# A decode kernel's first load, split between two issuing engines

## The chip, the cores and the metric

The kernel runs on one core of one Trainium2 chip, in float32. The metric is the device time of the program in microseconds (us). Engines are called by their names and by the profile's short ones: TensorE (PE), VectorE (DVE), ScalarE (ACT), GpSimd (POOL), SyncE (SP). Loads are issued by SyncE or ScalarE and are carried out by sixteen DMA engines that both share; in the profile SyncE's loads are on queue q1, ScalarE's on q10.

## The reference, cut to what matters

One token for each of two sequences goes through attention over a cache of 4096 positions (32 heads of 128) and, beside it, through an MLP; a gate mixes the two.

```python
# x (2,1,576), k_cache and v_cache (2,32,4096,128), wq (576,4096), wo (4096,576),
# w1 (576,4608), b1 (4608), w2 (4608,576), b2 (576), gate_w (576)
g = sigmoid((x * gate_w).sum(-1, keepdims=True))
q = (x @ wq).reshape(B, 1, 32, 128).transpose(0, 2, 1, 3)
p = softmax(einsum("bhqd,bhkd->bhqk", q, k_cache) * 128 ** -0.5)
a = einsum("bhqk,bhkd->bhqd", p, v_cache).transpose(0, 2, 1, 3).reshape(B, 1, 4096) @ wo
b = gelu(x @ w1 + b1) @ w2 + b2          # tanh form of gelu
return g * a + (1 - g) * b
```

Each of the caches is 134 MB and each of its bytes is used once.

## The kernel before, in words

Three buffers of on-chip memory, `slots[0]`, `slots[1]` and `slots[2]`, hold 128 partitions of 64 KB each, 8 MB a buffer. All large loads go through them, and all of them are issued by SyncE in one hand-written order. A small class, `Order`, writes the waits: `op` and `dma` take the keys that an instruction reads (`r`) and writes (`w`), and wait for the last semaphore value of each key; `o.wrote` remembers it. A load raises its semaphore by 16 when all of it has landed.

At the start, ScalarE issues four small loads: x (two rows, key `xg`), gate_w (one row beside x, `gt_in`), b1 (`b1T`, 144 B in each of 128 partitions) and b2 (`b2r`, one row). SyncE meanwhile issues five large ones: the first 512 rows of wq into slot 0 (key `s0`; partition p takes rows 4p to 4p+3, which is one contiguous run of 64 KB), the last 64 rows of wq into the end of slot 1 (`s1q`), and w1 in three parts into slots 1 and 2 (`s1a`, `s2a`, `s2h`).

GpSimd makes an identity matrix. VectorE, when x and gate_w are there, copies a part of them (L176); TensorE transposes x and gate_w (`turn`, L183); VectorE writes `xq`, `xT` and `gT` from the result (L190 to L193). TensorE then runs, in this order: the gate's products (`gate`, L198), q from slot 0 (`q_whole`, L241, reads `xq` and `s0`), q from the last rows (`q_half`), b2's part of the output (`bias2`, L267), and the MLP's first layer (L282, L291). VectorE and ScalarE finish the MLP's activation (L300 to L314).

SyncE's next load, the first K tile in two halves (`k_load(0)`), goes into slot 0 and so waits until TensorE is through with `q_whole`; the second K tile, into slot 1, waits for the MLP's products, the first V tile, into slot 2, for the rest of the MLP.

The main loop has sixteen steps (2 sequences x 8 groups of 4 heads). In each, VectorE multiplies the K tile by q (L353) and sums (L355), takes the maximum (L356 to L358), ScalarE takes the exponentials (L365), TensorE multiplies by the V tile (L384). K tiles alternate between slots 0 and 1, V tiles use slot 2; each load is issued as soon as its slot is free. After the loop w2 and wo come through the same slots, in seven loads; the semaphores of the early loads, listed in `early`, are used a second time there (value 32). TensorE adds their products (L473), VectorE copies (L492), TensorE adds the last rows of wo (L506), VectorE copies once more (L510) and the output is stored.

Of the kernel before, what the change touches and what calls it, by code (L numbers as in the profile page):

```python
# [8 lines left out]
PE = mybir.EngineType.PE  # L9
# [3 lines left out]
class Order:  # L13
# [50 lines left out]
    def op(self, e, f, r=(), w=(), extra=(), sig=None):  # L64

        self.wait(e, self.deps(r, w) + list(extra))
        ins = f(self.eng[e])
        if sig is not None:
            ins.then_inc(sig, 1)
            return None  # L70
        self.count[e] += 1
        ins.then_inc(self.sem[e], 1)
        t = self.token(e, self.sem[e], self.count[e])
        self.note(t, r, w)
        return t

    def dma(self, e, out, in_, r=(), w=(), extra=(), sem=None, val=16):
        self.wait(e, self.deps(r, w) + list(extra))
        if sem is None and self.spare:
            sem, val = self.spare.pop(0)  # L80
        elif sem is None:
            sem = self.tc.alloc_semaphore(f"d{self.nd}")
            self.nd += 1
        self.eng[e].dma_start(out, in_).then_inc(sem, 16)  # L84
        t = (None, sem, val, dict(self.seen[e]))
        self.note(t, r, w)
        return t


def kernel(tc, *args):  # L90
    with tc.tile_critical():
        stored = body(tc, *args)

    with tc.tile_critical():
        for own, sem, val, had in stored:
            tc.nc.sync.wait_ge(sem, val)


def body(tc, x, k_cache, v_cache, wq, wo, w1, b1, w2, b2, gate_w, out):
# [3 lines left out]
    F = w1.shape[1]  # L103
# [5 lines left out]
    NX = D // P  # L109
    XR = NX * P  # L110
    WQ = H * DH
# [6 lines left out]
    DW = D // 2  # L118
    SCALE = float(DH) ** -0.5
    SLOT = R * DH  # L120
    N1 = NQ - 1

    def sb(name, *shape):
        return nc.alloc_sbuf_tensor(name, list(shape), F32).ap()

    slots = [sb(f"slot{i}", P, SLOT) for i in range(3)]
    bank = [nc.alloc_psum_tensor(f"bank{i}", [P, 512], F32).ap() for i in range(8)]
# [3 lines left out]
    o = Order(tc)  # L131
    op, dma = o.op, o.dma
    S2 = ["s2a", "s2h", "s2r", "s2t", "xg", "b2r", "xe", "g1z"]


    b1T = sb("b1T", P, FR)
    spare = slots[2][:, 2 * F + 2 * FJ:]
    xg, spare = spare[:B + 1, :D], spare[:, D:]
    b2r, spare = spare[:1, :D], spare[:, D:]
# [1 line left out]
    dma("ACT", xg[B:B + 1], gate_w[None, :], w=["gt_in"])  # L141
    dma("ACT", b1T, b1.rearrange("(p r) -> p r", r=FR), w=["b1T"])
    dma("ACT", b2r, b2[None, :], w=["b2r"])


    hrow1 = w1[:XR].rearrange("(p r) n -> p (r n)", r=NX)
    wqh = slots[1][:, SLOT - WQ // 2:]
    FA = 3
    dma("SP", slots[0], wq[:XR].rearrange("(p r) n -> p (r n)", r=NX), w=["s0"])
    dma("SP", wqh, wq[XR:].rearrange("q (e n) -> (q e) n", e=2), w=["s1q"])  # L150
    dma("SP", slots[1][:, :FA * F], hrow1[:, :FA * F], w=["s1a"])
    dma("SP", slots[2][:, :F], hrow1[:, FA * F:], w=["s2a"])
    w1h = slots[2][:, F:F + F // 2]
    dma("SP", w1h, w1[XR:].rearrange("q (e n) -> (q e) n", e=2), w=["s2h"])
    early = [o.wrote[k][0][1] for k in ("xg", "gt_in", "b1T", "b2r", "s0", "s1q", "s1a", "s2a", "s2h")]
    hr = slots[2][:, 2 * F:2 * F + FJ]
    ht = slots[2][:, 2 * F + FJ:2 * F + 2 * FJ]

    def quad(src, i):
        g, b = divmod(i, B)  # L160
        return src[b, g * HQ:(g + 1) * HQ].rearrange("h (p r) d -> (h p) (r d)", p=HP)
# [26 lines left out]
    xq = sb("xq", P, NC6, B)  # L188
# [67 lines left out]
            ins = q_mm(e, NX + s, wqh, s, True)  # L256
        return ins

    op("PE", q_whole, r=["xq", "s0"], w=["q"])
    op("PE", q_half, r=["xq", "s1q"], w=["q"])  # L260


# [12 lines left out]
    def mlp_whole(lo, hi):  # L275
        def f(e):
            for c in range(lo, hi):
                t = slots[1][:, c * F:(c + 1) * F] if c < FA else slots[2][:, :F]
                for m in range(3):
                    for j in range(4):  # L280
                        at = j * FJ + m * FC
                        ins = e.matmul(hps[m][32 * j:32 * j + 32, :FC], xT[:, c], t[:, at:at + FC],  # L282
                                       start=(c == 0), stop=False, skip_group_check=True)
            return ins
        return f
# [8 lines left out]

    op("PE", mlp_whole(0, FA), r=["xT", "s1a"], w=["avp", "cps", "fin"])
    op("PE", mlp_whole(FA, NX), r=["xT", "s2a"], w=["avp", "cps", "fin"])
    op("PE", mlp_half, r=["xT", "s2h"], w=["avp", "cps", "fin"])

    for m, k in enumerate(("avp", "cps", "fin")):
# [5 lines left out]
       r=["s2r0", "s2r1", "s2r2"], w=["s2t"])  # L305
# [29 lines left out]
    def k_load(i):  # L335
        s = i % 2
        if i == 0:
            free = o.deps([], ["s0"])
            for a, sem in ((0, ksem[0]), (1, k0b)):
                c = slice(a * RH * DH, (a + 1) * RH * DH)  # L340
                dma("SP", slots[0][:, c], quad(k_cache, 0)[:, c], w=[f"s0{a}"], extra=free, sem=sem)
            return
        w = ["s0"] if s == 0 else ["s1a", "s1q", "s1"]
        dma("SP", slots[s], quad(k_cache, i), w=w, sem=ksem[s], val=16 * (i // 2 + 1))
# [15 lines left out]
    def soft(i):  # L360
        j = i % 2
        o.wait("ACT", o.deps([f"nm{j}", f"st{j}"], ["pt", "rs"]))
        for h in range(HQ):
            a = slice(HP * h, HP * (h + 1))
            ins = nc.scalar.activation(pt[a, h:R * HQ:HQ], stt[j][a], AF.Exp, bias=nmt[j][a], accum_out=rs[a])  # L365
        ins.then_inc(exps, 1)

    def gather(i):

        g, b = divmod(i, B)  # L370
        j = i % 2
        nc.scalar.wait_ge(avd, i + 1)
        nc.scalar.copy(avs, avp).then_inc(avc, 1)  # L373
        a = slice(32 * (g // 2), 32 * (g // 2) + 32)
        nc.scalar.wait_ge(cmb, i + 1)

        op("ACT", lambda e: e.copy(oS[a, b, g % 2], cps[a, :DH + 1]), r=[f"st{j}", f"nm{j}"], w=[f"oS{i}"])  # L377

    def quad_products(e, v, vin):
        e.wait_ge(exps, 1).then_inc(exps, -1)  # L380
        e.wait_ge(vin, 16).then_inc(vin, -16)  # L381
        for t in range(NT):
            j = t % 4
            ins = e.matmul(avp[32 * j:32 * j + 32], pt[:, 16 * t:16 * t + 32], v[:, 512 * t:512 * (t + 1)],  # L384
                           start=(t < 4), stop=(t >= NT - 4))
        ins.then_inc(avd, 1)
        e.wait_ge(avc, 1).then_inc(avc, -1)  # L387
        for rr in range(4):
            e.matmul(cps[:, :DH], sel[:, rr], avs[:, rr * DH:(rr + 1) * DH],  # L389
                     start=(rr == 0), stop=(rr == 3), skip_group_check=True)  # L390
        e.matmul(cps[:, DH:DH + 1], hsel, rs, start=False, stop=True, skip_group_check=True).then_inc(cmb, 1)  # L391


    WA = SLOT // D
    views = {"w2": w2.rearrange("(p r) n -> p (r n)", r=FR), "wo": wo.rearrange("(p r) n -> p (r n)", r=OR)}
# [7 lines left out]


    k_load(0)
    k_load(1)
    o.wait("SP", o.deps([], S2 + ["gt_in", "s2r0", "s2r1", "s2r2"]))
    nc.sync.dma_start(slots[2], quad(v_cache, 0)).then_inc(vin, 16)
    for i in range(NQ):
        qk(i)  # L410
        if i < NQ - 2:
            k_load(i + 2)
        elif i < N1:

            o.wait("SP", o.deps([], ["s0"]))
            nc.sync.dma_start(slots[0], quad(v_cache, N1)).then_inc(vlast, 16)
        soft(i)
        if i < N1:
            gather(i)
            nc.sync.wait_ge(avd, i + 1)  # L420
            if i < NQ - 2:
                nc.sync.dma_start(slots[2], quad(v_cache, i + 1)).then_inc(vin, 16)
    o.wait("PE", o.deps(["sel0", "sel1", "sel2", "sel3", "hsel", "pt"], ["avp", "cps"]))
    with nc.Fori(0, N1, engines=[PE], head_slot={PE: 0}):
        quad_products(nc.tensor, slots[2], vin)
    quad_products(nc.tensor, slots[0], vlast)
    gather(N1)

# [19 lines left out]
    for gp in range(2):  # L448
# [11 lines left out]
       r=["orr", "rg"], w=["oT"])  # L460
# [82 lines left out]
```

## Time and profile before

| | us |
|---|---|
| median of 3 runs (723.55 to 723.66) | 723.56 |
| the profiled execution | 723.58 |
| its span in the profile | 721.7 |
| VectorE busy | 573.1 |
| TensorE busy | 223.1 |
| ScalarE busy | 49.5 |

The span runs from the first to the last thing that the profile shows; the rest of the execution's time lies around it. The profile's DMA row gives, in 40 equal slices of the span or of a window, the mean busy share of the sixteen DMA engines in tenths; the GB/s row counts a packet's bytes in the slice in which it starts. A packet is one contiguous piece that one DMA engine moves; a 64 KB run is one packet. In section 3 the last figure of a queue is the time of its packets as a share of sixteen engines over the stretch. A row of the timeline gives start, duration, engine, line and operation, and in brackets how long the engine had been idle and what released it. Nearly all loads are issued from one line of the helper `Order.dma` (L84), so they are told apart by their tensors.

### The profile page before, as it was taken

Reading aid. Unit: us, or ns where it says so; the run is one execution under the profiler, and the core shown is the slowest. Engines: PE = TensorE matmul, PEld = TensorE weight load, DVE = VectorE, ACT = ScalarE, POOL = GpSimd, SP = SyncE. Lnnn points to the kernel's source line nnn. Section 1 sums busy time; section 2 is a strip of 40 time slices with the busy share of each in tenths; the row PEclk is TensorE's granted clock in tenths of the full one; section 3 lists DMA queues with packets and bytes.
Section 4 is the critical chain, followed back from the end, with each engine's and each line's share of the span. In section 5 each row is a group of like instructions: output and inputs, shape, how many; then the busy total and the mean of one; then the engine's idle time right before and its main releaser. Section 6 shows DMA issues by size and latency. Waiting matters only on the chain. (4 is left out here: it accounts for less than half of the span.)

```text
span 721.7 us, 4080 instructions
## 1 busy us (share of the span) xinstructions
PE 223.1 (31%) x1784; PEld 80.2 (11%) x1784; DVE 573.1 (79%) x124; ACT 49.5 (7%) x166; POOL 0.7 (0%) x6
## 2 busy tenths in 40 slices
PE   1790005050504032140505060504032130506556
PEld 1130002010101010010101020201001010102112
DVE  2007999999989898989899898989898989899100
ACT  0000010101010101010100001010101010100100
POOL 0000000000000000000000000000000000000000
PEclk9996557575666657575757575656657575757759
DMA  9999999999999999999999999999999999999996
GB/s 408 412 411 455 418 454 418 454 418 454 414 444 429 432 432 421 447 421 450 421 447 425 443 425 443 421 432 436 421 450 421 447 425 447 421 443 429 434 407 278
DMA packets 6656, 308.69 MB, mean 428 GB/s; under 512 B 876, under 2 KB 884, under 8 KB 1016
## 3 DMA queue, kind: packets, MB, share of 16 engines
q1 hardware_dynamic: 6488, 308.55, 99.0%
q8 instruction: 6, 0.10, 0.1%
q10 hardware_dynamic: 160, 0.03, 0.0%
q14 instruction: 2, 0.02, 0.0%
HBM read 308.57 MB, written 0.00 MB: 428 GB/s over the span
## 5 line engine op out<-in xcount | busy, mean ns | idle before, releaser
L353 DVE TENSOR_TENSOR slot<-slot,bank 128x16384 f32<-128x16384 f32 (+1 forms) x17 | 275.7, 16215 | 43.4 <-DMA slot<-in_A_k_cache_dram 43.4
L384 PE MATMUL bank<-slot,pt 128*32 128x512 f32 x1024 | 146.1, 735 | 448.4 <-PEq L381 448.4
L355 DVE TENSOR_REDUCE st<-slot 128x128 f32<-128x16384 f32 x16 | 275.5, 17220 | 0.6
L384 PEld LDWEIGHTS bank<-slot,pt 128*32 128x32 f32 x1024 | 40.2, 132 | 541.8 <-issue 541.8
L365 ACT ACTIVATE pt<-st,nm 32x128 f32<-32x128 f32 x64 | 33.0, 515 | 115.5 <-DVE nm L358 114.7
L373 ACT COPY avs<-bank 128x512 f32<-128x512 f32 x16 | 9.4, 585 | 437.7 <-PE bank L384 437.7
L304 DVE STREAM_TRANSPOSE slot<-slot 128x1152 f32<-128x1152 f32 x1 | 2.2, 2205 | 37.5 <-ACT slot L300 37.5
L492 DVE COPY pt<-bank 128x288 f32<-128x288 f32 x1 | 0.5, 458 | 31.3 <-PE bank L473 31.3
L241 PE MATMUL bank<-slot,xq 128*32 128x512 f32 x160 | 20.2, 669 | 7.9 <-DMA slot<-in_A_wq_dram 7.9
L389 PE MATMUL bank<-avs,sel 128*128 128x128 f32 x128 | 18.1, 284 | 12.7 <-PEq L387 12.7
L389 PEld LDWEIGHTS bank<-avs,sel 128*128 128x128 f32 x128 | 15.5, 191 | 26.8 <-issue 26.8
L473 PE MATMUL bank<-slot,hg 128*2 128x288 f32 x144 | 12.0, 478 | 8.4 <-DMA slot<-in_B_w_dram 8.4
L365 ACT ACTIVATION_READ_ACCUMULATOR pt<-st,nm 32x1 f32 x64 | 12.5, 195 | 0.0
L449 DVE TENSOR_TENSOR avs<-oS,dm 128x256 f32<-128x256 f32 x2 | 0.8, 422 | 14.5 <-ACT oS L377 14.5
L473 PE MATMUL bank<-slot,oT 128*2 128x288 f32 x108 | 9.9, 516 | 4.8 <-DMA slot<-in_A_wo_dram 4.8
L282 PE MATMUL bank<-slot,xT 128*32 128x384 f32 x96 | 7.9, 487 | 0.0
L241 PEld LDWEIGHTS bank<-slot,xq 128*32 128x32 f32 x160 | 5.2, 121 | 22.1 <-issue 14.1
L176 DVE COPY slot<-slot 3x64 f32<-3x64 f32 x2 | 0.4, 184 | 8.9 <-DMA slot<-in_gate_w_dram 8.9
L473 PEld LDWEIGHTS bank<-slot,hg 128*2 128x2 f32 x144 | 4.0, 95 | 15.5 <-DMA slot<-in_B_w_dram 8.4
L377 ACT COPY oS<-bank 32x129 f32<-32x129 f32 x16 | 4.1, 258 | 22.9 <-PE bank L391 22.9
L356 DVE TENSOR_REDUCE mx<-st 128x1 f32<-128x128 f32 x16 | 4.6, 286 | 0.5
L391 PEld LDWEIGHTS bank<-rs,hsel 128*128 128x128 f32 x32 | 4.9, 192 | 0.0
(59 smaller groups left out, 43.0 us busy)
## 6 DMA issues: line engine op xcount, KB each, us to landing
slot<-in_A_k_cache_dram SPq DMA_DIRECT2D x2, 4096.0 KB, 25.8
slot<-in_B_w_dram SPq DMA_DIRECT2D x1, 8064.0 KB
slot<-in_B_w_dram SPq DMA_DIRECT2D x1, 6912.0 KB, 41.0
slot<-in_B_w_dram SPq DMA_DIRECT2D x2, 2304.0 KB, 25.4
slot<-in_A_wo_dram SPq DMA_DIRECT2D x1, 4032.0 KB
slot<-in_A_wo_dram SPq DMA_DIRECT2D x1, 2304.0 KB
slot<-in_A_wo_dram SPq DMA_DIRECT2D x1, 1440.0 KB, 33.5
slot<-in_B_w_dram SPq DMA_DIRECT2D x1, 1152.0 KB
```

The lines of the kernel that those rows point to most:

```text
L241: ins = e.matmul(qps[b][m][HP * h:HP * (h + 1)], xq[:, c, b:b + 1].to_broadcast([P, HP]), v[:, :, h], start=(c == 0), stop=last, skip_grou ...
L282: ins = e.matmul(hps[m][32 * j:32 * j + 32, :FC], xT[:, c], t[:, at:at + FC], start=(c == 0), stop=False, skip_group_check=True)
L353: op(V, lambda e, lo=lo, hi=hi: e.tensor_mul(k[:, lo:hi], k[:, lo:hi], q.unsqueeze(1).to_broadcast([P, hi - lo, DH])), r=["q", key], w=[key])
L355: op(V, lambda e: e.tensor_reduce(stt[j], k, AX.X, ALU.add), r=[s] + [p[2] for p in parts], w=[f"st{j}"])
L356: op(V, lambda e: e.tensor_reduce(mxt, stt[j], AX.X, ALU.max), r=[f"st{j}"], w=["mx"])
L365: ins = nc.scalar.activation(pt[a, h:R * HQ:HQ], stt[j][a], AF.Exp, bias=nmt[j][a], accum_out=rs[a])
L373: nc.scalar.copy(avs, avp).then_inc(avc, 1)
L377: op("ACT", lambda e: e.copy(oS[a, b, g % 2], cps[a, :DH + 1]), r=[f"st{j}", f"nm{j}"], w=[f"oS{i}"])
L384: ins = e.matmul(avp[32 * j:32 * j + 32], pt[:, 16 * t:16 * t + 32], v[:, 512 * t:512 * (t + 1)], start=(t < 4), stop=(t >= NT - 4))
L389: e.matmul(cps[:, :DH], sel[:, rr], avs[:, rr * DH:(rr + 1) * DH], start=(rr == 0), stop=(rr == 3), skip_group_check=True)
L391: e.matmul(cps[:, DH:DH + 1], hsel, rs, start=False, stop=True, skip_group_check=True).then_inc(cmb, 1)
L473: ins = e.matmul(acc[64 * s + 32 * u:64 * s + 32 * u + B], lhs[:, r], wrow[name, r][0][:, u * DW:(u + 1) * DW], start=False, stop=r >= hi ...
```

## The change

ScalarE's first instruction is now a load of wq: partitions 0 to 15 of slot 0, sixteen runs of 64 KB (key `s0f`). SyncE loads the other 112 runs (key `s0`). x, gate_w, b1 and b2 follow on ScalarE behind the wq runs, in the same order as before. The large loads are written ahead of the small ones in the program; SyncE's order of its own is the same. `q_whole` and the first K load wait on both keys, and the semaphore of `s0f` comes first in the list of those used again at the end.

```diff
+    NE = 16
...
+    hrow1 = w1[:XR].rearrange("(p r) n -> p (r n)", r=NX)
+    wqh = slots[1][:, SLOT - WQ // 2:]
+    FA = 3
+
+    hrowq = wq[:XR].rearrange("(p r) n -> p (r n)", r=NX)
+    dma("ACT", slots[0][:NE], hrowq[:NE], w=["s0f"])
+    dma("SP", slots[0][NE:], hrowq[NE:], w=["s0"])
+    dma("SP", wqh, wq[XR:].rearrange("q (e n) -> (q e) n", e=2), w=["s1q"])
...
     dma("ACT", xg[:B], x.rearrange("b s d -> (b s) d"), w=["xg"])
     dma("ACT", xg[B:B + 1], gate_w[None, :], w=["gt_in"])
     dma("ACT", b1T, b1.rearrange("(p r) -> p r", r=FR), w=["b1T"])
     dma("ACT", b2r, b2[None, :], w=["b2r"])
-    hrow1 = w1[:XR].rearrange("(p r) n -> p (r n)", r=NX)
-    wqh = slots[1][:, SLOT - WQ // 2:]
-    FA = 3
-    dma("SP", slots[0], wq[:XR].rearrange("(p r) n -> p (r n)", r=NX), w=["s0"])
-    dma("SP", wqh, wq[XR:].rearrange("q (e n) -> (q e) n", e=2), w=["s1q"])
...
-    early = [o.wrote[k][0][1] for k in ("xg", "gt_in", "b1T", "b2r", "s0", "s1q", "s1a", "s2a", "s2h")]
+    early = [o.wrote[k][0][1] for k in ("s0f", "xg", "gt_in", "b1T", "b2r", "s0", "s1q", "s1a", "s2a", "s2h")]
...
-    op("PE", q_whole, r=["xq", "s0"], w=["q"])
+    op("PE", q_whole, r=["xq", "s0f", "s0"], w=["q"])
...
     def k_load(i):
         s = i % 2
         if i == 0:
-            free = o.deps([], ["s0"])
+            free = o.deps([], ["s0f", "s0"])
```

More of the change, by code (lines that the diff above doesn't have):

```diff
@@ L133, in body @@
     S2 = ["s2a", "s2h", "s2r", "s2t", "xg", "b2r", "xe", "g1z"]
+    hrow1 = w1[:XR].rearrange("(p r) n -> p (r n)", r=NX)
[5 more added lines that the diff above has]
+    dma("SP", wqh, wq[XR:].rearrange("q (e n) -> (q e) n", e=2), w=["s1q"])
+    dma("SP", slots[1][:, :FA * F], hrow1[:, :FA * F], w=["s1a"])
+    dma("SP", slots[2][:, :F], hrow1[:, FA * F:], w=["s2a"])
+    w1h = slots[2][:, F:F + F // 2]
+    dma("SP", w1h, w1[XR:].rearrange("q (e n) -> (q e) n", e=2), w=["s2h"])
     b1T = sb("b1T", P, FR)
@@ L143, in body @@
     dma("ACT", b2r, b2[None, :], w=["b2r"])
-    hrow1 = w1[:XR].rearrange("(p r) n -> p (r n)", r=NX)
-    wqh = slots[1][:, SLOT - WQ // 2:]
-    FA = 3
-    dma("SP", slots[0], wq[:XR].rearrange("(p r) n -> p (r n)", r=NX), w=["s0"])
-    dma("SP", wqh, wq[XR:].rearrange("q (e n) -> (q e) n", e=2), w=["s1q"])
[L151 to L154, printed above, removed]
-    early = [o.wrote[k][0][1] for k in ("xg", "gt_in", "b1T", "b2r", "s0", "s1q", "s1a", "s2a", "s2h")]
+    early = [o.wrote[k][0][1] for k in ("s0f", "xg", "gt_in", "b1T", "b2r", "s0", "s1q", "s1a", "s2a", "s2h")]
     hr = slots[2][:, 2 * F:2 * F + FJ]
```

## The prediction

> **What bounds the kernel now.** The page comes first: the profiled execution took 723.58 us, 0.02 above the median of the runs (723.56), 1.88 of it outside the span. The sum below is made against 723.58.
>
> ```profile
> span 721.7 us, 4080 instructions
> ...
> DMA  9999999999999999999999999999999999999996
> ...
> q1 hardware_dynamic: 6488, 308.55, 99.0%
> ...
> HBM read 308.57 MB, written 0.00 MB: 428 GB/s over the span
> ```
>
> The sixteen DMA engines are full from the first slice to the last but one, and q1, SyncE's queue, carries nearly every byte. VectorE, busiest of the compute engines, waits for K inside its main loop (view of waits), and the chain that ends last is a load, three short steps ahead of the output:
>
> ```profile
> DVE slot L353 <- DMA slot<-in_A_k_cache_dram: 43.4, 14, 3.4
> ```
> ```profile
> 680.76 35.82 DMA slot<-in_A_wo_dram
> ...
> 716.62 1.45 PE bank L506 x40
> ...
> 718.10 0.31 DVE pt L510
> ```
>
> So the kernel is a stream of bytes: it ends when the slowest DMA engine has moved its share. One engine moves 428/16 = 26.75 GB/s, and a 64 KB run takes it 65,536 B / 26.75 GB/s = 2.45 us. Since the queue never empties, an engine that starts earlier ends earlier, and an engine held up in the first load is late to the end. The start, in 20 ns slices (window 1.80 to 2.60), and what was issued:
>
> ```profile
> GB/s 0 0 230 0 0 0 0 0 0 13107 3277 0 0 0 3277 0 6554 6554 0 3277 0 3277 0 0 0 0 3277 0 3277 0 0 0 3277 0 0 0 0 0 3277 0
> ...
> q1 hardware_dynamic: 16, 1.05, 390.7%
> ```
> ```profile
> 0.91 0.55 ACTq L84 DMA_DIRECT2D slot<-in_A_x_dram  x1
> ...
> 0.95 0.86 SPq L84 DMA_DIRECT2D slot<-in_A_wq_dram  x2
> ...
> 2.61 1.28 ACT L204 ACT_TABLE_LOAD   x1 [2.61 <-issue]
> ```
>
> A packet counts in the slice where it starts: 3277 GB/s is one 64 KB run, 13107 four, 230 the two packets of x. ScalarE's x is issued at 0.91 and starts at 1.85, 0.94 later; SyncE's wq is issued at 0.95 and its first runs start at 1.98, the sixteenth engine's at 2.55. Those first runs take 3.907 x 0.80 x 16 / 16 = 3.13 us each, 0.68 over the steady 2.45.
>
> **The change, part by part.** (1) The start. If ScalarE's sixteen runs come 0.94 us after 0.91, they start at 1.85: 0.13 us sooner for the first engine, 0.70 for the last. If its issue is the slower one (x's took 0.55, the two on SyncE 0.86/2 = 0.43 each), SyncE's runs simply go first, as now. Bounds 0 and -0.70; I take **-0.30**, nearer to the mean than to the last engine.
>
> (2) The shape of the loads, which is the part that decides. Before, every large load covers 128 partitions, eight runs for each engine. After, sixteen engines write at one time into sixteen neighbouring partitions, and SyncE's 112 runs are seven for each engine. No row of before shows a large load narrower than 128. If 26.75 GB/s belongs to the engine, the sixteen runs cost 2.45 us whatever their address: 0. If it belongs to the memory side in proportion to partitions, sixteen of them get 428 x 16/128 = 53.5 GB/s, and 1.05 MB takes 19.6 us: +17.2. Between the ends lie two engines to one entrance (+2.45) and four (+7.35). The nearest rows are small ones, x (two engines, partitions 0 and 1, at once) and gate_w (one engine alone, with one packet of b1 in its window):
>
> ```profile
> q10 hardware_dynamic: 3, 0.00, 23.4%
> ```
> ```profile
> q10 hardware_dynamic: 2, 0.00, 4.2%
> ```
>
> The first window is 0.15 us long (from 1.80), the second 0.16 (from 7.80). x's packets took 0.234 x 16 x 0.15 = 0.56 us, gate's 0.042 x 16 x 0.16 = 0.11: five times as much for the pair, 2.6 times for each packet. It could be the cold start alone, since the first wq runs, on 128 partitions, are 0.68 over their steady time too; that is why the free end keeps a chance. I take a factor of 4, between 2.6 and 5: **+7.35 us**, both ends kept. [...]
>
> (3) SyncE's 112 runs. [...] One shared run costs 2.45, all seven 17.2. I take one: **+2.45**.
>
> Nothing behind makes these up: the bytes are the same, and the stretch from 60 to 400 us already runs full.
>
> ```profile
> 40.00:50.00 10.00, 10.00 (x108) 3.75 (x104) 0.00 (x0) 0.00 (x0) 0.00 (x0) 1.00 0.96 405
> ...
> 60.00:400.00 340.00, 83.02 (x592) 29.63 (x592) 316.17 (x47) 25.36 (x88) 0.00 (x0) 0.62 1.00 434
> ```
>
> (The last two columns are the DMA share and GB/s.)
>
> (4) x, gate_w, b1 and b2 behind the run on ScalarE's queue. Who waits:
>
> ```profile
> 10.79 0.40 DVE L176 COPY slot<-slot 3x64 f32<-3x64 f32 x2 [8.88 <-DMA slot<-in_gate_w_dram]
> ...
> 12.84 2.29 PE L198 MATMUL bank<-xT,gT 128*128 128x2 f32 x10 [0.74 <-DVE gT L193]
> 15.17 0.17 ACT L204 ACTIVATE gb<-bank 128x2 f32<-128x2 f32 x1 [11.27 <-PE bank L198]
> ...
> 17.85 0.21 DVE L233 TENSOR_TENSOR fsel<-ident 128x2 f32<-128x2 f32 x2
> 23.04 20.18 PE L241 MATMUL bank<-slot,xq 128*32 128x512 f32 x160 [7.91 <-DMA slot<-in_A_wq_dram]
> ...
> 39.86 10.86 SPq L84 DMA_DIRECT2D slot<-in_A_k_cache_dram  x3
> ...
> 55.54 2.21 DVE L304 STREAM_TRANSPOSE slot<-slot 128x1152 f32<-128x1152 f32 x1 [37.47 <-ACT slot L300]
> ...
> 59.61 0.23 DVE L314 TENSOR_TENSOR hg<-gt,g 128x72 f32<-128x72 f32 x1
> 60.84 8.69 DVE L353 TENSOR_TENSOR slot<-slot,bank 128x8192 f32<-128x8192 f32 x1 [1.00 <-DMA slot<-in_A_k_cache_dram]
> 70.86 8.69 DVE L353 TENSOR_TENSOR slot<-slot,bank 128x8192 f32<-128x8192 f32 x1 [1.33 <-DMA slot<-in_A_k_cache_dram]
> ```
>
> Small packets alternate with SyncE's runs on an engine. gate_w gets four entries ahead of it: the run, its semaphore, x and x's semaphore, 4 x 2.45 = 9.8 us at full rate. L176 moves from 10.79 to 20.6, and TensorE, which does the gate's products before q and is through with them 12.84 + 2.29 - 10.79 = 4.34 us after L176 starts, is ready for q at 24.9 instead of waiting from 15.13 for wq at 23.04: 1.9 late. With the runs shared, the run ahead costs 9.8 alone and one shared round 2.45: L176 at 10.79 + 9.8 + 7.35 + 2.45 = 30.4, TensorE ready at 34.7, wq there at 23.04 + 9.5 = 32.5, 2.2 late. The cover: K is issued at 39.86, when q's matmuls have freed slot 0, while wq and w1, all issued by 3.5 us, are 9.44 + 10.62 = 20.06 MB and keep the engines busy to 2.0 + 46.9 = 48.9. K may come 9 us later before a DMA engine idles. On VectorE the MLP ends 1.00 us ahead of the first half of K, and the second half is waited for by another 1.33, so 2.3 us late is absorbed there. I cost it at 0; without the cover, 1.9 to 2.2 us. VectorE's other work of the start (10.79 to 18.06) moves along and has until 55 us. b1 and b2 go later by the same entries; b2 is read after q, past 43 us, b1 after the MLP.
>
> (5) Instructions. One DMA issue more on ScalarE (0.24 to 0.55 us): the table load moves from 2.61 to 3.2 at most, its use is at 15.17 and moves later. One wait more ahead of q on TensorE, hidden as above. K's wait is on the same token of TensorE. The semaphores reused at the end shift by one place in the list: 0. The load of w2 and wo keeps its shape.
>
> **Sum:** 723.58 - 0.30 + 7.35 + 2.45 + 0 = 733.08, **733.1 us**, 1.3% slower.
>
> **The rivals.** (a) Not slower: addresses cost nothing, the engines are the limit. For it: the steady rate is one figure per engine in every stage of the stream, and x's slow pair has a second explanation. Against it: nothing wide could show the difference. Time: 723.58 - 0.30 = 723.3, within 722.9 and 723.6. The point that decides is whether the first sixteen runs take 3.1 us or near 10. [...]
>
> (b) The runs are shared, but less: SyncE's first runs get between ScalarE's on half the engines, so that two, not four, meet at a time over two rounds, and the 112 do not collide. 2 x 2.45 = 4.9: 723.58 - 0.30 + 4.9 = 728.2. For it: 0.91 and 0.95 are only 0.04 apart, so the order on each engine is open. Against it: x did come 0.13 sooner than wq.
>
> (c) The gate's chain runs past its cover: more than 9 us beyond the load's own delay, as when each small entry waits for two runs instead of one (7.35 more, still under 9). Each us above counts in full; 736 at 3 us more. Against it: gate_w and its semaphore came through by 10.79 with three runs ahead of them.
>
> (d) Faster by over 0.2%: 1.45 us is twice all that the start has to give (0.70).
>
> **How the numbers follow.** 0.2% of 723.56 is 1.45 us, about what a measurement of this kernel can tell from no change. The forecast, shared runs with some collisions among the 112 (729 to 737), has 0.53; (b), 725 to 729, 0.17; (a) 0.25; (c) 0.03; (d) 0.02. Slower: 0.53 + 0.17 + 0.03 = 0.73; same 0.25; faster 0.02. The range reaches from (a), 723.0, to the forecast's upper part, 737.0 (ScalarE's runs +7.35 and about two and a half shared runs, 6.1, each engine); the forecast's own range is 729 to 737.
>
> **What would show it.** In the profile of after: step 1, the slice in which the first 64 KB runs start (1.85 right, 1.98 wrong); step 2, the share of q10's sixteen runs (65,536 B at 3.1 us each would refute the sharing, near 10 confirm it) and GB/s over 2 to 20 us (near 410 or under 300); step 3, wq's landing, 23.04 before at the first L241, near 32.5 forecast, near 30 if the 112 do not collide; step 4, L176's start at 20 to 31 and a DMA share near 1 from 40 to 60 us in spite of it. The prediction is wrong if the first L241 starts near 23 us, or if the delay at L241 does not reappear at the end.

## The result, and the profile after

The changed kernel took 744.50 us (median of 4 runs, 743.98 to 744.95) against 723.61 for the kernel before (four runs beside it): ratio 1.0288, 95% interval 1.0275 to 1.0301. The forecast, 733.1, had the sign and the place of the loss, wq's arrival, but less than half of its size: 9.5 us were summed and 20.9 measured.

The page of the changed kernel, its span, DMA, GB/s and HBM rows:

```profile
span 742.9 us, 4082 instructions
...
DMA  9989999999999999999999999999999999999996
GB/s 169 265 347 418 445 434 434 430 438 438 427 434 431 434 434 434 430 434 434 430 441 427 430 445 427 427 445 427 427 448 427 434 438 430 434 434 434 428 413 262
...
HBM read 308.57 MB, written 0.00 MB: 415 GB/s over the span
```

The same bytes, and DMA engines that look as busy as before; only the GB/s row tells that in the first two slices (37 us) they move 169 and 265 where the later ones move some 430. A busy share counts a packet that is held up as busy. The timeline of the first 62 us has the delay where TensorE starts on q, and the chain that ends last has it again, unchanged, at the end:

```profile
37.84 0.40 DVE L180 COPY slot<-slot 3x64 f32<-3x64 f32 x2 [35.93 <-DMA slot<-in_gate_w_dram]
...
44.32 17.88 PE L245 MATMUL bank<-slot,xq 128*32 128x512 f32 x152 [2.14 <-DMA slot<-in_A_wq_dram]
...
59.68 0.80 SPq L84 DMA_DIRECT2D slot<-in_A_k_cache_dram  x2
```
```profile
737.84 1.45 PE bank L510 x40
```

wq is there at 44.32 instead of 23.04, 21.28 us later; the last products start at 737.84 instead of 716.62, 21.22 later. Nothing, on balance, was lost or won in between.

Now the runs by themselves. A *round* is the sixteen runs, one for each DMA engine, that are under way together. Three windows of the DMA view: 1.9 to 3.2 us (the first run of each engine), 6.4 to 8.5 (the second), 14.8 to 40 (the other six, with b1's small packets); a packet counts with its whole time in the window in which it starts:

```profile
q1 hardware_dynamic: 16, 1.05, 374.3%
```
```profile
q10 hardware_dynamic: 16, 1.05, 424.5%
```
```profile
q1 hardware_dynamic: 96, 6.29, 102.5%
```

Share x window x 16 / packets gives the mean of a run. SyncE's runs came first on every engine and took 3.743 x 1.3 = 4.87 us (3.13 before). ScalarE's sixteen were second, at 4.245 x 2.1 = 8.91 us each. The six that follow took 1.025 x 25.2 x 16 / 96 = 4.31. Against the steady run of before (window 4.9 to 20.1, which holds 7.27 MB or 111 packets),

```profile
q1 hardware_dynamic: 111, 7.27, 110.4%
```

1.104 x 15.2 x 16 / 111 = 2.42 us, the loss of an engine is 1.74 + 6.49 + 6 x 1.89 = 19.6 us: 6.5 from ScalarE's sixteen partitions, 13.1 from SyncE's 112. The other 1.7 us to the delay at L245 was not traced; a mean does not tell which engine finishes last.

### The profile page after: what moved, and what is told of

Read it like the earlier page. It is cut to its first block, busy times and chain, and to the rows that moved or that the text cites. A ratio compares the mean times of both kernels' runs of the same rounds, so it can differ in the third digit from the quotient of the medians.

```text
span 742.9 us, 4082 instructions
## 1 busy us (share of the span) xinstructions
PE 226.1 (30%) x1784; PEld 81.8 (11%) x1784; DVE 573.0 (77%) x124; ACT 49.5 (7%) x166; POOL 0.7 (0%) x6
## 5 line engine op out<-in xcount | busy, mean ns | idle before, releaser
L388 PE MATMUL bank<-slot,pt 128*32 128x512 f32 x1024 | 150.1, 752 | 445.7 <-PEq L385 445.7
L180 DVE COPY slot<-slot 3x64 f32<-3x64 f32 x2 | 0.4, 184 | 36.0 <-DMA slot<-in_gate_w_dram 35.9
L245 PE MATMUL bank<-slot,xq 128*32 128x512 f32 x160 | 18.7, 630 | 2.1 <-DMA slot<-in_A_wq_dram 2.1
L453 DVE TENSOR_TENSOR avs<-oS,dm 128x256 f32<-128x256 f32 x2 | 0.8, 422 | 15.2 <-ACT oS L381 15.2
L477 PE MATMUL bank<-slot,oT 128*2 128x288 f32 x108 | 10.1, 528 | 4.2 <-DMA slot<-in_A_wo_dram 4.2
L245 PEld LDWEIGHTS bank<-slot,xq 128*32 128x32 f32 x160 | 5.7, 116 | 14.4 <-issue 14.4
```

Of the source, the lines that this page charges most:

```text
L245: ins = e.matmul(qps[b][m][HP * h:HP * (h + 1)], xq[:, c, b:b + 1].to_broadcast([P, HP]), v[:, :, h], start=(c == 0), stop=last, skip_grou ...
L477: ins = e.matmul(acc[64 * s + 32 * u:64 * s + 32 * u + B], lhs[:, r], wrow[name, r][0][:, u * DW:(u + 1) * DW], start=False, stop=r >= hi ...
```

## The experiments

The theories call an *entrance* a group of partitions of on-chip memory whose writers would share one rate; no trace shows one. Three theories. **A**: the address in on-chip memory decides; runs that enter by the same partitions at one time share a rate. **B**: the address in main memory decides. **C**: two queues that alternate on each DMA engine cost the time. The kernel before took 723.45 to 723.60 us beside them (medians, each on the same chip). Only the first experiment was run more than once; the others differ from the kernel before by 4 us or more, and its own runs by 1.4 us at most.

**Both queues, full width.** ScalarE loads the first 16 KB of every partition's run, SyncE the other 48 KB; the rest is as in the changed kernel.

```diff
-    dma("ACT", slots[0][:NE], hrowq[:NE], w=["s0f"])
-    dma("SP", slots[0][NE:], hrowq[NE:], w=["s0"])
+    dma("ACT", slots[0][:, :WQ], hrowq[:, :WQ], w=["s0f"])
+    dma("SP", slots[0][:, WQ:], hrowq[:, WQ:], w=["s0"])
```

> ScalarE's first instruction loads wq's first 16 KB for all 128 partitions, SyncE the other 48 KB; the small loads stay behind on ScalarE. Theory A (addresses in on-chip memory: runs that go to the same few partitions at one time share one engine's rate): no sharing at 128 partitions, so the 21 us go away: 723.0 to 724.0 us, wq there (first L245) near 23 us. Theory B (addresses in main memory: reading pieces closer together or further apart slows the engines): the source is now pieces of 16 KB and 48 KB, 64 KB apart; some loss, over 2 us. Theory C (two queues alternating on each DMA engine cost the time): most of the loss stays, 735 us or more. All: gate_w comes late, q with it, by under 9 us, and that costs nothing.

Measured 723.74 us (11 runs, 723.64 to 723.99); ratio to the kernel before 1.0001, interval 0.9992 to 1.0010. The whole loss is gone with both queues at work, so C falls. Nothing is won either. ScalarE's load is here the first to start (window 1.80 to 2.60):

```profile
GB/s 0 0 0 0 0 0 0 0 0 1638 2458 0 0 819 0 1638 0 819 1638 0 819 0 0 819 0 819 0 0 0 0 0 0 0 0 0 0 0 0 0 0
...
q10 hardware_dynamic: 14, 0.23, 138.3%
```

A 16 KB packet is 819 GB/s in a slice: its packets begin at 1.98, the time at which SyncE's began before. It also shows the gate's chain late and without a price (timeline, 0 to 45); q does not wait for wq here, so its start is not wq's arrival, as the expectation had it:

```profile
23.89 0.40 DVE L180 COPY slot<-slot 3x64 f32<-3x64 f32 x2 [21.99 <-DMA slot<-in_gate_w_dram]
...
28.17 17.05 PE L245 MATMUL bank<-slot,xq 128*32 128x512 f32 x144
```
```profile
43.58 10.86 SPq L84 DMA_DIRECT2D slot<-in_A_k_cache_dram  x3
```

q starts 5.1 us after the 23.04 of before, K is issued 3.7 us later, and the time is the same.

**One queue, the same shapes.** SyncE alone issues 16 partitions, then 112; the small loads stand where they did. In this edit and the later ones that split wq, not shown: `q_whole` and the first K load wait for all of the new keys, and `early` lists them.

```diff
-    dma("SP", slots[0], wq[:XR].rearrange("(p r) n -> p (r n)", r=NX), w=["s0"])
+    dma("SP", slots[0][:16], hrowq[:16], w=["s0f"])
+    dma("SP", slots[0][16:], hrowq[16:], w=["s0"])
```

> SyncE alone issues both parts, 16 partitions and then 112; the small loads are where they were before. A: the loss stays, 741 to 746 us, with wq there near 43 us; gate_w near 11 to 20 us. B: the same, 741 to 746. C: the loss goes, 723 to 725. It shows the 112 partitions alone behind the 16, without a second queue: under A and B its runs take 4 to 5 us as in the changed kernel; if the changed kernel's 112 were slow only because they alternated with the other queue, they take 2.4 and the time is near 731.

745.74 us, with q's products starting at 45.37: the loss needs no second queue. The sixteen, now first (window 1.9 to 3.2), take 6.591 x 1.3 = 8.57 us, the cold start included (3.13 for the first runs of the kernel before, where later ones take 2.42), and the 112 (window 8 to 37, 98 packets by 6.42 MB) 0.942 x 29 x 16 / 98 = 4.46:

```profile
q1 hardware_dynamic: 16, 1.05, 659.1%
```
```profile
q1 hardware_dynamic: 114, 6.42, 94.2%
```

**Eight loads of sixteen partitions**, in three arrangements of the destination and one of the source (in the last, rows of wq go to other partitions than q's products take them for). At the 6.49 us that ScalarE's sixteen cost in the changed kernel, eight loads of neighbours cost 52 us more, 775.5; at the prediction's factor of 4, an estimate, 8 x 3 x 2.42 = 58 more, 781.7.

```diff
-    dma("SP", slots[0], wq[:XR].rearrange("(p r) n -> p (r n)", r=NX), w=["s0"])
+    for a in range(8):   # one of:
+        dma("SP", slots[0][16 * a:16 * a + 16], hrowq[16 * a:16 * a + 16], w=[S0[a]])   # neighbours
+        dma("SP", slots[0][a::8], hrowq[a::8], w=[S0[a]])                               # eight apart
+        dma("SP", slots[0][c], hrowq[c], w=[S0[a]])      # four apart: c = slice(64*(a//4) + a%4, 64*(a//4) + 64, 4)
+        dma("SP", slots[0][16 * a:16 * a + 16], hrowq[a::8], w=[S0[a]])                 # neighbours, source 8 apart
```

> wq as eight loads of SyncE, each sixteen neighbouring partitions, sources neighbouring too. [...] C: 724 to 727 (eight issues instead of one).

> wq as eight loads of SyncE, each sixteen partitions eight apart, sources 512 KB apart. A, with entrances shared by neighbours: half the crowding or none, 2 runs to an entrance: 8 x 2.42 = 19.3 us more, 743 us; 724 if sixteen partitions eight apart have an entrance each. If the number of partitions in a load counts and not which, the same as with sixteen neighbours, 770 to 782. B: depends on the source step; 724 if closeness was the cause.

> wq's runs are put into other partitions (q is not the reference's): sixteen neighbouring partitions as the destination of each of eight loads, the sources 512 KB apart. A: as eight loads of sixteen neighbours with neighbouring sources, 770 to 782 us. B: as eight loads with partitions eight apart, whose sources are the same as here.

> wq as eight loads of SyncE, each sixteen partitions four apart within one half (0, 4, ..., 60 and so on). A, if an entrance belongs to four neighbours alone: sixteen entrances, no loss, 724 to 727 us. [...]

| sixteen partitions | source | us | over 723.5 |
|---|---|---|---|
| neighbours | neighbours | 779.0 | 55.5 |
| neighbours | eight apart | 778.1 | 54.6 |
| eight apart | eight apart | 744.9 | 21.4 |
| four apart, in one half | four apart | 744.7 | 21.2 |

The first two differ in the source only and agree; the second and third differ in the destination only and are 33 us apart. So A, and B falls. The mean run of the first three, from the windows 9 to 68, 9 to 68 and 7 to 38 (112, 112 and 106 large packets by their MB, in the order of the table):

```profile
q1 hardware_dynamic: 224, 7.34, 111.3%
```
```profile
q1 hardware_dynamic: 224, 7.34, 110.5%
```
```profile
q1 hardware_dynamic: 209, 6.95, 108.5%
```

1.113 x 59 x 16 / 112 = 9.38 us, 9.31, and 1.085 x 31 x 16 / 106 = 5.08: 3.9 and 2.1 times 2.42. It is not the number of partitions that counts but which. By the 1.05 MB of such a load, sixteen neighbours get 1.05 MB / 9.38 us = 112 GB/s and sixteen eight apart 206, where the full width gets 433 (2.42 us). Four apart in one half is no better than eight apart (744.7 and 744.9 us): the 724 to 727 us of an entrance for every four neighbours did not come. Which partitions get in each other's way was not shown beyond these arrangements.

**Why the 112 are so dear.** Two theories were tried for SyncE's part. **F**: only the engines that meet at an entrance go slower. **L**: one crowded entrance slows all sixteen. The first two kernels leave SyncE's wq whole and add five loads of 4 x 12 KB, never used, at the head of ScalarE's queue (such a load is what the expectations speak of; the crowded loads go to four neighbouring partitions, the spread ones to four that are twelve apart); the third splits wq into 96 partitions and 32, on SyncE.

```diff
+    for a in range(5):   # crowd: four neighbours; spread: 64 + a:101 + a:12
+        dma("ACT", slots[2][64 + 8 * a:68 + 8 * a, 13184:13184 + 3072], w1[4 * a:4 * a + 4, :3072], w=[f"dum{a}"])
...
-    dma("SP", slots[0], wq[:XR].rearrange("(p r) n -> p (r n)", r=NX), w=["s0"])
+    dma("SP", slots[0][:96], hrowq[:96], w=["s0"])        # the third kernel
+    dma("SP", slots[0][96:], hrowq[96:], w=["s0f"])
```

> [...] SyncE's loads keep their full width. Theory L (while an entrance is crowded, all sixteen engines go slower): every engine's 64 KB runs of wq that meet such a load are held up to 4 x 0.45 = 1.8 us; the mean of the 128 runs rises from 2.46 us to 3 us or more, and wq is there 3 to 7 us later than 23.04. [...]

> [...] L: mean of wq's 128 runs 2.6 to 2.8 us, clearly under that of the crowded loads. [...]

> SyncE loads wq as 96 partitions (six runs an engine) and 32 (two). L: some entrance is used twice in every round, so every engine goes at half rate in all eight: 8 x 2.66 = 21 us, 743 to 746 us. [...]

The three took 730.4, 727.8 and 743.8 us. 96 + 32 is L's number (743 to 746; the entrance used twice in every round is assumed there, not shown), and its runs are slow throughout (window 7 to 37, 97 large packets by their MB: 1.008 x 30 x 16 / 97 = 4.99 us):

```profile
q1 hardware_dynamic: 113, 6.36, 100.8%
```

For the spread loads the rounds of the stream can be told apart; q1 in the windows 7.4 to 8.5, with four 12 KB packets in it, and 10.1 to 11.1, with none:

```profile
q1 hardware_dynamic: 16, 1.05, 244.5%
q10 hardware_dynamic: 4, 0.05, 10.7%
```
```profile
q1 hardware_dynamic: 16, 1.05, 243.1%
q10 hardware_dynamic: 16, 0.00, 1.3%
```

The sixteen runs took 2.445 x 1.1 = 2.69 us in the mean in the first, 2.43 in the second. Had each 12 KB packet held up one run and no other, which is the author's estimate for F and not shown, the mean could have risen by a quarter of one such packet (0.107 x 1.1 x 16 / 4 = 0.47 us), to 2.55. In a later round with such packets (window 12.6 to 13.2) twelve runs took 3.637 x 0.6 x 16 / 12 = 2.91 us:

```profile
q1 hardware_dynamic: 12, 0.79, 363.7%
```

For the crowded loads, the windows 10.8 to 12 and 14.2 to 15.3:

```profile
q1 hardware_dynamic: 11, 0.72, 196.7%
```
```profile
q1 hardware_dynamic: 10, 0.66, 139.5%
```

1.967 x 1.2 x 16 / 11 = 3.43 us where three 12 KB packets start while the runs are under way (between 12.06 and 13.02, by the GB/s row of the window 4.9 to 24), 1.395 x 1.1 x 16 / 10 = 2.46 where one does (at 14.475). Narrow windows take the eleven apart, 11.3 to 11.65 with five runs and 11.735 to 11.742 with one:

```profile
q1 hardware_dynamic: 5, 0.33, 299.9%
```
```profile
q1 hardware_dynamic: 1, 0.07, 3750.9%
```

One run took 37.509 x 0.007 x 16 = 4.20 us, 1.78 over the free 2.42; the profile doesn't name its engine. The five took 2.999 x 0.35 x 16 / 5 = 3.36, 0.94 over, and the other five, by what is left of 11 x 3.43, 3.35 in the mean. So each part of the eleven was late in the mean, ten runs by about half of what the one was, while three packets came. Over all of wq the means were 2.89 and 2.60 us (windows 4.9 to 24 and 4.9 to 22): just under L's 3 for the crowd, and the low end of its 2.6 to 2.8 for the spread loads. How many engines meet a 12 KB packet is not shown; with one for each, F's 2.55 stands against 2.69, and F falls on that estimate alone. wq's landing can't be read from q's start there, since x and gate_w behind the added loads came later still. What makes the others wait was not found.

No arrangement beat the kernel before, and the nearest, the full-width split, is its equal.

## Why the prediction was wrong, point by point

**What bounds the kernel**: right. A delay of 21.28 us at wq came out as 21.22 at the last products, and the loss as 20.9.

**(1) The start, -0.30 summed: 0.** ScalarE's sixteen-engine load does not start 0.94 us after its issue, as x's two packets did: in the full-width split it was issued at 0.92 and started at 1.98, 1.06 later. In the changed kernel SyncE's runs came first, which is the step's other bound; q10 shows no packet before 2.60, and the row of that window has SyncE's only:

```profile
q1 hardware_dynamic: 15, 0.98, 566.2%
```

**(2) Sixteen partitions, +7.35: right, and partly by luck.** 6.49 in the changed kernel, 6.96 a load in the kernel of eight (9.38 - 2.42). A factor of 3.7 to 3.9, where 4 was taken. The row it was drawn from, x's slow pair, did not carry it. Taken one by one in the kernel before (windows 1.850 to 1.855 and 1.855 to 1.860), x's packets are not alike:

```profile
q10 hardware_dynamic: 1, 0.00, 113.8%
```
```profile
q10 hardware_dynamic: 1, 0.00, 577.5%
```

They took 0.09 and 0.46 us, and gate_w's, alone, 0.09 by the same reading (window 7.850 to 7.855): one of the pair was not slowed at all, so 2.6 and 5 were no bounds for a shared rate. The 128-partition rows of before left the question open, and the free end (rival a) was as consistent with them.

**(3) SyncE's 112, +2.45: this step failed.** It cost 13.1. The step priced one shared run in seven for each engine, and no run shows that share. What the runs showed in its place is that all seven rounds were slow, in part or in full: 4.87, then 5.08, 3.65, 3.34, 4.46, 4.70 and 4.60 (windows 14.8 to 18, 20.5 to 22.5, 24.2 to 25.8, 27.4 to 29.3, 31.6 to 33.7 and 36.2 to 38.5), 4.31 in the mean, where sixteen partitions eight apart cost 5.08. The runs of 96 + 32 were slow throughout too (4.99), and beside the crowded loads eleven runs took 3.43 in the mean while three 12 KB packets came. Even in the quickest, six runs (window 24.2 to 24.4) took 5.936 x 0.2 x 16 / 6 = 3.17 and not 2.42:

```profile
q1 hardware_dynamic: 6, 0.39, 593.6%
```

The bound "all seven, 17.2" stood in the text and was not taken into the range, which ended at two and a half. Why some of SyncE's rounds are quicker than 5.08 is open: the profile doesn't say which engine carries which partition.

**(4) The gate's chain, 0: right.** L180 moved to 37.84 (30.4 forecast), since the runs ahead of gate_w were slower than summed, and TensorE was ready for q at 42.18 = 44.32 - 2.14, before wq and not 2.2 us behind it as forecast, since wq was later still. K was issued at 59.68, and the stream stayed full (the rows for 45 to 60 and 60 to 70 us).

Small packets did alternate with SyncE's runs: in the window 20.5 to 22.5 sixteen of 4 B start on q10 beside sixteen runs, x's two follow a round later, at 24.26 and 24.46, and gate_w's two rounds behind them, at 32.18. In the kernel before it is sixteen and sixteen as well (window 7.4 to 8.06). The rows of 20.5 to 22.5, of 7.4 to 8.06, and of the stream:

```profile
q1 hardware_dynamic: 16, 1.05, 182.4%
q10 hardware_dynamic: 16, 0.00, 0.8%
```
```profile
q1 hardware_dynamic: 16, 1.05, 366.4%
q10 hardware_dynamic: 16, 0.00, 2.9%
```
```profile
45.00:60.00 15.00, 15.00 (x136) 4.75 (x132) 0.11 (x2) 0.00 (x0) 0.00 (x0) 1.00 1.01 435
60.00:70.00 10.00, 10.00 (x112) 3.73 (x104) 0.00 (x0) 0.00 (x0) 0.00 (x0) 1.00 0.94 396
```

The full-width split, where the chain alone makes q 5.1 us late, is the clean test of it.

**(5) Instructions, 0**: nothing in the trace speaks against it.

**The rivals.** (a) would have been right if addresses cost nothing; the 779.0 and 744.9 us of two loads of equal size refute it. A second issuing engine by itself won nothing: 723.74 against 723.60. (b) had SyncE's runs ahead of ScalarE's on half of the engines; they were ahead on all, and ScalarE's sixteen took 8.91 us each, 3.7 times 2.42 where (b) had twice, and the 112 were slow too, 4.31 us each. (c) and (d) did not occur.

## What to carry to other kernels

A large load that is to be split is better split along its columns than along its partitions: here 128 partitions for each piece cost nothing (ratio 1.0001), and 16 + 112 cost 2.9%. Read GB/s beside the busy share of the DMA engines, since held-up packets count as busy (here 169 GB/s in a slice that is 90% busy or more). And when a shared resource might be crowded, price the case in which everybody waits for it, not only those who meet there.

## What the runs showed of the hardware

- A 64 KB run took 2.42 us in a load of 128 partitions (kernel before, window 4.9 to 20.1), 5.08 in loads of sixteen partitions eight apart, and 9.38 and 9.31 in loads of sixteen neighbours, whose source addresses were 64 KB and 512 KB apart.
- Beside 12 KB packets of other loads the runs of wq took longer: 2.69 us instead of 2.43 in the mean of sixteen while four such packets started (spread loads), 2.91 for twelve in a later round; while three started that went to neighbouring partitions, 4.20 for one run of eleven, 3.36 in the mean of five, 3.35 in the mean of the rest (crowded loads).
- ScalarE's sixteen-engine load, issued at 0.92, starts at 1.98 (full-width split), like SyncE's, issued at 0.95 and started at 1.98 (kernel before); x's load of two packets, issued at 0.91, started at 1.85.
